# Fused retention and gated feed-forward: chunks taken two batch elements at a time, column-tiled Y and state, all inputs by software DMA

## The chip, the cores and the metric

The kernel runs on one core of one Trainium2 chip. The metric is device time in microseconds (us), the median of several executions (an execution over 1.5% above the fastest of its kernel counts as slow). A profile shows one execution, and its span (first to last instruction) is about 1.8 us shorter than the time of that execution.

Engines: PE does matmuls (PEld is its weight load), DVE, ACT and POOL (GpSimd) do elementwise work, SP (SyncE) issues DMAs. POOL also issues DMAs: the "software queue", as against SP's "hardware queue".

## The reference

```python
# q, k, v: (batch 4, heads 8, seq 768, head_dim 64) float32
gamma = 1.0 - 2.0 ** (-5.0 - np.arange(H))
for t in range(S):
    state = gamma * state + einsum('bhd,bhe->bhde', k[:, :, t], v[:, :, t])
    y[:, :, t] = scale * einsum('bhd,bhde->bhe', q[:, :, t], state)
x = y.transpose(0, 2, 1, 3).reshape(B * S, H * D)      # 3072 x 512
h = x @ w_in                                           # 512 -> 2048
out = (h * np.cos(h)) @ w_out                          # 2048 -> 512
```

Both kernels cut a sequence into 6 chunks of 128 positions. Within a chunk they form the masked scores of q and k, multiply by v and add what the 64x64 state of each head gives. The decay is folded into a scaling of q and of v by powers of gamma. There are 24 chunks; four of them make a 512-row group for the feed-forward part, so there are six groups.

## The kernel before

Per chunk: scale q (DVE) and v (POOL), transpose q and k on PE, scores, mask (DVE), Y, state. The stages of a chunk are issued between blocks of four feed-forward matmuls, one chunk per four blocks in and four blocks out ("[... ]" marks a cut):

```python
def load_chunk(ci):                 # k: software queue, cast to bf16; q, v: hardware queue
    for eng, t, src in ((nc.gpsimd, ks, k), (nc.sync, qf, q), (nc.sync, vf, v)):
        eng.dma_start(out=t[s], in_=src[b, :, ds(c * C, C)].rearrange("h t d -> t h d"))

def conv(ci):                       # qs = q * gq on DVE; vp = v * gk on POOL, zero-padded to 128 columns
    nc.vector.tensor_tensor(out=qs[n], in0=qf[s], in1=bc(gq), op=ALU.mult)
    nc.gpsimd.tensor_tensor(out=vout, in0=vf[s]..., in1=gk[...], op=ALU.mult)

def stage_y(ci):                    # 3 full-width matmuls for each pair of heads
    for a in range(HP):
        if c > 0:
            nc.tensor.matmul(yp[:, a, :], lhsT=stb[ci % 2][:, a, :], rhs=sq[ci % 3][:, 0, a, :], ...)
        for j in range(2):
            nc.tensor.matmul(yp[:, a, :], lhsT=vp[n][:, a, j, :], rhs=am[ci % 2][j][:, a, :], ...)

for g in range(NG + 1):
    for s in range(16):
        k4, r = divmod(s, 4)
        if g < NG: unit_f(g, s)               # 4 matmuls, Sin on ACT, multiply on DVE
        if g > 0:  unit_o(g - 1, k4, r)       # 4 matmuls
        ci = (g + 1) * GT + k4
        if ci < NT:
            if r == 0:   conv(ci); stage_t(ci)      # scaling and transposes in the same block
            elif r == 1: stage_a(ci)                # scores, mask
            elif r == 3: stage_y(ci); stage_s(ci); [... load_chunk(ci + GT)]
```

## Time and profile before

| | |
|---|---|
| Time | 276.5 us (276.05 to 278.29, 4 runs) |
| Span of the profile | 273.2 us |
| Start, to the first feed-forward matmul | 29.65 us |
| Group 0 (feed-forward-in and the attention of group 1) | 35.0 us |
| Groups 1 to 4 (in, out and attention) | 163.3 us, 20.4 us per two chunks |
| Tail (no attention left) | 45.2 us |

Lines of the page of the kernel before: span, busy time of each engine, and the span in 40 slices (a digit is the busy share in tenths; PEclk is the granted clock of PE), two DMA queues (packets, MB, share of 16 engines) and the engine shares of the chain of waits that ended last (followed back from the last instruction, at each step to what released it).

```profile
span 273.2 us, 3823 instructions
PE 217.3 (80%) x1480; PEld 111.6 (41%) x1504; DVE 129.1 (47%) x224; ACT 119.3 (44%) x172; POOL 53.6 (20%) x64
PE   0347469667988987988987988987988988999994
PEclk9999997989999999999999999999999999999999
DMA  9999999999275275175275274044000000100011
q1 hardware_dynamic: 53376, 18.88, 30.9%
q0 software_dynamic: 29184, 7.34, 27.1%
PE 67%; DVE 10%; ACT 8%; issue 3%; ACTq 0%; DVEq 0%
```

PE carries the chain, but its slices read 9, 8, 7: it pauses at a steady rhythm. DMA is saturated for the first ten slices (68 us) and only partly busy after that.

The stage table of the kernel before: a stretch, its length, then busy time of each engine in it, granted clock, DMA share (above 1 where packets overlap), GB/s.

```profile
0.00:29.65 29.65, 11.34 (x124) 9.11 (x125) 13.52 (x35) 8.08 (x12) 17.70 (x27) 1.00 1.31 193
29.65:64.65 35.00, 24.28 (x181) 12.28 (x185) 19.75 (x34) 18.40 (x25) 12.53 (x14) 0.90 1.38 180
64.65:227.96 163.31, 140.27 (x988) 71.53 (x1004) 84.73 (x141) 77.12 (x112) 23.41 (x24) 1.00 0.41 74
227.96:273.20 45.24, 41.39 (x188) 18.71 (x191) 11.06 (x16) 15.67 (x24) 0.00 (x0) 1.00 0.14 53
```

In groups 1 to 4 PE is idle for 163.31 - 140.27 = 23.0 us. The timeline of one chunk there (start, length, engine, line, instruction, and in brackets the idle time before it with what ended it) shows where:

```profile
126.67 0.69 ACT L212 ACTIVATE cosb_126<-bank_66,halfpi 128x512 bf16<-128x512 f32 x1 [0.50 <-PE bank_66 L209]
127.39 0.69 DVE L213 TENSOR_TENSOR gt_122<-bank_66,cosb_126 128x512 bf16<-128x512 f32 x1 [0.71 <-ACT cosb_126 L212]
128.00 0.68 DVE L138 TENSOR_TENSOR qs_107<-qf_87,gq 128x512 bf16<-128x512 f32 x1
128.74 0.40 PE L153 MATMUL bank_68<-ident,qs_107 128*128 128x128 bf16 x4 [1.24 <-DVE qs_107 L138]
```

DVE ran these in the order of issue. The scaling of q (L138) is issued behind the multiplication of the feed-forward block just begun (L213), which waits for that block's Sin (L212). So the transposes (L153) wait 1.24 us in every chunk, though this q had landed long ago, at 99.07 us.

Two lines of POOL's timeline at the start of the kernel before:

```profile
30.33 0.75 POOL L109 DMA_DIRECT2D w_out_sb<-in_moe_w_out_dram  x1 [0.61 <-DMA w_in_sb<-in_moe_w_in_dram]
32.78 0.95 POOL L101 DMA_DIRECT2D ks_89<-in_k_dram  x1 [0.64 <-DMA ks_93<-in_k_dram]
```

In these programs a software DMA waits until the eighth software DMA before it has landed (the built program uses eight completion semaphores in turn). No software DMA is issued before that landing, and the waits mostly end 0.3 us after it: in these two lines w_in had landed at 30.05 us and the k load at 32.49. The wait sits in POOL's own instruction stream, so POOL's elementwise work behind it waits too.

### The profile page before, as it was taken

What the parts mean: (1) busy time and instruction counts of PE and PEld (TensorE: products, weight loads), DVE (VectorE), ACT (ScalarE), POOL (GpSimd) and SP (SyncE); (2) the same over time, 40 slices, a digit from 0 to 9 for tenths busy, and PEclk for the clock granted to TensorE, in tenths of its full rate; (3) what the DMA queues carried; (4) which work ended last, traced back from release to release, by engine and by line L of the source; (5) the groups of instructions that cost most, each with busy time, mean ns of one, the idle gap of its engine ahead of it and who ended that gap; (6) DMA issues with size and microseconds to landing.
All of it is one profiled execution on the core that took longest, in us unless ns stands there. A gap on an engine that the chain in (4) does not pass through costs nothing.

```text
span 273.2 us, 3823 instructions
## 1 busy us (share of the span) xinstructions
PE 217.3 (80%) x1480; PEld 111.6 (41%) x1504; DVE 129.1 (47%) x224; ACT 119.3 (44%) x172; POOL 53.6 (20%) x64
## 2 busy tenths in 40 slices
PE   0347469667988987988987988987988988999994
PEld 0235234334534533434534534434534534444441
DVE  2636474556555553555554553654554653333200
ACT  2222455543544543544543644544544544444311
POOL 7527822225022022022012021101100000000000
PEclk9999997989999999999999999999999999999999
DMA  9999999999275275175275274044000000100011
GB/s 140 197 216 222 168 190 196 169 167 148 20 134 115 22 136 122 15 134 120 22 129 121 18 134 115 19 100 115 13 27 38 32 9 38 41 38 38 38 77 77
DMA packets 82577, 26.45 MB, mean 97 GB/s; under 512 B 75392, under 2 KB 79488, under 8 KB 82560
## 3 DMA queue, kind: packets, MB, share of 16 engines
q1 hardware_dynamic: 53376, 18.88, 30.9%
q0 software_dynamic: 29184, 7.34, 27.1%
q8 instruction: 11, 0.18, 0.3%
q14 instruction: 6, 0.05, 0.1%
HBM read 27.26 MB, written 6.29 MB: 123 GB/s over the span
## 4 chain that ended last, share of the span: by engine, by line
PE 67%; DVE 10%; ACT 8%; issue 3%; ACTq 0%; DVEq 0%
PE bank_69 L223 6%; PE bank_68 L209 5%; PE bank_65 L209 5%; PE bank_64 L209 5%; PE bank_67 L223 4%; PE bank_63 L223 4%; PE bank_66 L209 4%; PE bank_63 L209 4%; PE bank_67 L209 3%; PE bank_69 L209 3%; PE bank_65 L223 3%; PE bank_64 L223 3%; DVE gt_122 L213 3%; PE bank_66 L223 3%; ACT cosb_124 L212 3%
## 5 line engine op out<-in xcount | busy, mean ns | idle before, releaser
L209 PEld LDWEIGHTS <-w_in_sb 128*128 128x128 bf16 x384 | 34.9, 99 | 38.7 <-issue 7.2
L223 PEld LDWEIGHTS <-gt_122 128*128 128x128 bf16 x192 | 18.8, 98 | 22.6
L223 PEld LDWEIGHTS <-gt_123 128*128 128x128 bf16 x192 | 18.8, 98 | 22.7
L223 PE MATMUL bank_69<-w_out_sb,gt_122 128*128 128x512 bf16 x63 | 16.2, 379 | 0.1
L153 PEld LDWEIGHTS <-qs_105 128*128 128x128 bf16 x32 | 2.0, 106 | 25.3 <-DVE qs_105 L138 25.3
L223 PE MATMUL bank_63<-w_out_sb,gt_123 128*128 128x512 bf16 x48 | 11.8, 379 | 0.0
L223 PE MATMUL bank_64<-w_out_sb,gt_123 128*128 128x512 bf16 x48 | 11.8, 379 | 0.0
L209 PE MATMUL bank_68<-xt_121,w_in_sb 128*128 128x512 bf16 x40 | 10.8, 379 | 1.0 <-ACT xt_121 L202 0.7
L185 DVE CAST stb_119<-st_ps 64x256 bf16<-64x256 f32 x24 | 10.1, 421 | 2.8 <-PE st_ps L181 2.1
L209 PE MATMUL bank_64<-xt_121,w_in_sb 128*128 128x512 bf16 x42 | 10.9, 380 | 0.1
L209 PE MATMUL bank_66<-xt_120,w_in_sb 128*128 128x512 bf16 x36 | 10.1, 401 | 0.4 <-issue 0.3
L209 PE MATMUL bank_65<-xt_120,w_in_sb 128*128 128x512 bf16 x34 | 9.2, 385 | 0.6 <-ACT xt_120 L202 0.5
L212 ACT ACTIVATE cosb_126<-bank_66,halfpi 128x512 bf16<-128x512 f32 x8 | 5.5, 688 | 7.4 <-PE bank_66 L209 7.4
L209 PE MATMUL bank_69<-xt_120,w_in_sb 128*128 128x512 bf16 x33 | 8.6, 380 | 0.2
L209 PE MATMUL bank_65<-xt_121,w_in_sb 128*128 128x512 bf16 x31 | 8.2, 379 | 0.5 <-ACT xt_121 L202 0.5
L185 DVE CAST stb_118<-st_ps 64x256 bf16<-64x256 f32 x16 | 6.7, 421 | 3.7 <-PE st_ps L181 3.4
L223 PE MATMUL bank_67<-w_out_sb,gt_122 128*128 128x512 bf16 x31 | 8.2, 379 | 0.1
L223 PE MATMUL bank_65<-w_out_sb,gt_122 128*128 128x512 bf16 x32 | 8.2, 379 | 0.0
L223 PE MATMUL bank_67<-w_out_sb,gt_123 128*128 128x512 bf16 x32 | 8.2, 379 | 0.0
L223 PE MATMUL bank_66<-w_out_sb,gt_122 128*128 128x512 bf16 x32 | 8.2, 379 | 0.0
L153 PEld LDWEIGHTS <-qs_107 128*128 128x128 bf16 x32 | 1.9, 101 | 15.4 <-DVE qs_107 L138 15.4
L212 ACT ACTIVATE cosb_124<-bank_65,halfpi 128x512 bf16<-128x512 f32 x8 | 5.5, 688 | 6.2 <-PE bank_65 L209 6.2
(391 smaller groups left out, 491.7 us busy)
## 6 DMA issues: line engine op xcount, KB each, us to landing
w_in_sb<-in_moe_w_in_dram POOLq DMA_DIRECT2D x4, 512.0 KB, 8.9
w_out_sb<-in_moe_w_out_dram POOLq DMA_DIRECT2D x4, 512.0 KB, 18.1
out_dram<-ob_127 SPq DMA_DIRECT2D x6, 256.0 KB, 2.1
out_dram<-ob_128 SPq DMA_DIRECT2D x6, 256.0 KB, 2.1
out_dram<-ob_129 SPq DMA_DIRECT2D x6, 256.0 KB, 2.1
out_dram<-ob_130 SPq DMA_DIRECT2D x6, 256.0 KB, 2.1
qf_81<-in_q_dram SPq DMA_DIRECT2D x3, 256.0 KB, 3.4
vf_97<-in_v_dram SPq DMA_DIRECT2D x3, 256.0 KB, 4.2
```

Of the source, the lines that this page charges most:

```text
L153: nc.tensor.transpose(tr[:, w, a, :], src[:, 2 * a : 2 * a + 2, :], ident)
L185: nc.vector.tensor_copy(out=stb[(ci + 1) % 2][ts(j, 64), :, ts(j, 64)], in_=st_ps[ts(j, 64), :, ts(j, 64)])
L209: nc.tensor.matmul(bank, lhsT=w_in_sb[:, i, ts(f, 128)], rhs=xt[g % 2][:, i, :], start=(i == 0), stop=(i == KIN - 1))
L212: nc.scalar.activation(out=cb, in_=bank, func=AF.Sin, bias=halfpi)
L213: nc.vector.tensor_tensor(out=gt[g % 2][:, f, :], in0=bank, in1=cb, op=ALU.mult)
L223: nc.tensor.matmul(bank, lhsT=gt[g % 2][:, f, ts(j, 128)], rhs=w_out_sb[:, f, :], start=(f == 0), stop=(f == KOUT - 1))
```

## The change

The intent: handle the same chunk of two batch elements as one pair, so that each stage is issued once per eight blocks; spread the stages (transposes one block after scaling, Y four blocks after scores); write Y and state of the two heads of a pair into the two column halves of the array, so that they can run side by side without zero padding; and take q's scaling from DVE by giving it to POOL. q, k and v are now all loaded by POOL's software queue as float32; k is cast by DVE (by ACT for the first two pairs).

```diff
-    def load_chunk(ci):
-        for eng, t, src in ((nc.gpsimd, ks, k), (nc.sync, qf, q), (nc.sync, vf, v)):
-            eng.dma_start(out=t[s], in_=src[b, :, ds(c * C, C)]...)
+    def load_pair(p):
+        for t, src in ((qf, q), (kf, k), (vf, v)):
+            for b in range(2):
+                nc.gpsimd.dma_start(out=t[p % PRE][:, b], in_=src[2 * bp + b, :, ds(c * C, C)]...)
 [... stage_y: two half-width products for the state, two for v ...]
-                nc.tensor.matmul(yp[:, a, :], lhsT=stb[ci % 2][:, a, :], ...)
-                nc.tensor.matmul(yp[:, a, :], lhsT=vp[n][:, a, j, :], ...)
+                for j in range(2):
+                    nc.tensor.matmul(yp[ts(j, 64), a, :], lhsT=stb[p % 2][:, b, a, ts(j, 64)], ...)
+                for j in range(2):
+                    nc.tensor.matmul(yp[ts(j, 64), a, :], lhsT=vs[n][:, b, 2 * a + j, :], ...)
 [... state likewise: st_ps[ts(j, 64), b, a, :], 64 columns of 64 ...]
 [... start: two pairs loaded, w_in, the two pairs' attention, then: ...]
+    load_pair(2)
+    load_pair(3)
+    stage_y(1)
+    for r in range(4):
+        load_w_out(r)
+    load_pair(4)
+    def conv(p):
+        conv_q(p, nc.gpsimd)
+        conv_k(p, False)            # DVE
+        conv_v(p, nc.gpsimd)
 [... main loop, hf, r = divmod(s, 8) ...]
+                if r == 0:
+                    conv(p)
+                elif r == 1:
+                    stage_t(p)
+                elif r == 2:
+                    todo = stage_a(p)
+                    stage_m(p, todo[0])
+                elif r == 3:
+                    stage_m(p, todo[1])
+                elif r == 6:
+                    stage_y(p)      # and state
+                    if p + 3 < NP:
+                        load_pair(p + 3)
```

More of the change, by code (lines that the diff above doesn't have):

```diff
@@ L49 @@
     KOUT = DF // 128
-    GT = 4
-    NT = B * NC
-    NG = NT // GT
-    PRE = 8
+    NP = B // 2 * NC
+    NG = NP // 2
+    PRE = 5
     scale = 1.0 / math.sqrt(D)
@@ L67 @@
     banks = Banks([psum.tile([128, 512], FP32, name=f"bank{i}") for i in range(7)])
-    st_ps = psum.tile([128, HP, 128], FP32, name="st_ps")
+    st_ps = psum.tile([128, 2, HP, D], FP32, name="st_ps")
     ident = sb([128, 128], BF16, "ident")
@@ L80 @@
     w_out_sb = sb([128, KOUT, DM], BF16, "w_out_sb")
-    qf = [sb([128, H, D], FP32, f"qf{i}") for i in range(PRE)]
-    ks = [sb([128, H, D], BF16, f"ks{i}") for i in range(PRE)]
-    vf = [sb([128, H, D], FP32, f"vf{i}") for i in range(PRE)]
+    qf = [sb([128, 2, H, D], FP32, f"qf{i}") for i in range(PRE)]
+    kf = [sb([128, 2, H, D], FP32, f"kf{i}") for i in range(PRE)]
+    vf = [sb([128, 2, H, D], FP32, f"vf{i}") for i in range(PRE)]
     NB = 3
-    qs = [sb([128, H, D], BF16, f"qs{i}") for i in range(NB)]
-    vp = [sb([128, HP, 2, 128], BF16, f"vp{i}") for i in range(NB)]
-    sq = [sb([128, 2, HP, 128], BF16, f"sq{i}") for i in range(3)]
-    am = [[sb([128, HP, 128], BF16, f"am{i}_{j}") for j in range(2)] for i in range(2)]
-    stb = [sb([128, HP, 128], BF16, f"stb{i}") for i in range(2)]
-    xt = [sb([128, KIN, GT * C], BF16, f"xt{i}") for i in range(2)]
-    gt = [sb([128, KOUT, GT * C], BF16, f"gt{i}") for i in range(2)]
-    cosb = [sb([128, GT * C], BF16, f"cosb{i}") for i in range(3)]
-    ob = [sb([128, DM], FP32, f"ob{i}") for i in range(4)]
-    def load_chunk(ci):
-        b, c = divmod(ci, NC)
-        s = ci % PRE
-        for eng, t, src in ((nc.gpsimd, ks, k), (nc.sync, qf, q), (nc.sync, vf, v)):
-            eng.dma_start(out=t[s], in_=src[b, :, ds(c * C, C)].rearrange("h t d -> t h d"))
+    qs = [sb([128, 2, H, D], BF16, f"qs{i}") for i in range(NB)]
+    ks = [sb([128, 2, H, D], BF16, f"ks{i}") for i in range(NB)]
+    vs = [sb([128, 2, H, D], BF16, f"vs{i}") for i in range(NB)]
+    qkt = [sb([128, 2, 2, HP, 128], BF16, f"qkt{i}") for i in range(NB)]
+    am = [[[sb([128, HP, 128], BF16, f"am{i}_{b}_{j}") for j in range(2)]
+           for b in range(2)] for i in range(2)]
+    stb = [sb([128, 2, HP, 128], BF16, f"stb{i}") for i in range(2)]
+    xt = [sb([128, KIN, 4 * C], BF16, f"xt{i}") for i in range(2)]
+    gt = [sb([128, KOUT, 4 * C], BF16, f"gt{i}") for i in range(2)]
+    cosb = [sb([128, 4 * C], BF16, f"cosb{i}") for i in range(3)]
+    ob = [sb([128, DM], FP32, f"ob{i}") for i in range(4)]
+    def load_pair(p):
+        bp, c = divmod(p, NC)
+        for t, src in ((qf, q), (kf, k), (vf, v)):
+            for b in range(2):
+                nc.gpsimd.dma_start(
+                    out=t[p % PRE][:, b],
+                    in_=src[2 * bp + b, :, ds(c * C, C)].rearrange("h t d -> t h d"))
     def load_w_in(r):
@@ L111, in load_w_out @@
             in_=moe_w_out[ts(r, 512), :].rearrange("(f p) m -> p f m", p=128))
-    for ci in range(GT):
-        load_chunk(ci)
     nc.gpsimd.iota(pos, pattern=[[C, NC]], base=1, channel_multiplier=1,
                    allow_small_or_imprecise_dtypes=True)
+    load_pair(0)
+    make_identity(nc, ident)
     nc.vector.memset(lnsc, math.log(scale))
     nc.vector.memset(halfpi, math.pi / 2.0)
+    nc.vector.memset(mask, 1.0)
     for h in range(H):
@@ L125 @@
     nc.scalar.activation(out=gk, in_=lgp, func=AF.Exp, scale=-1.0)
-    make_identity(nc, ident)
-    nc.vector.memset(mask, 1.0)
     nc.gpsimd.affine_select(out=mask, in_=mask, compare_op=ALU.is_ge, fill=0.0,
                             base=0, pattern=[[1, 128]], channel_multiplier=-1)
-    for t in vp + stb:
+    for t in stb:
         nc.vector.memset(t, 0.0)
-    def conv(ci):
-        c = ci % NC
-        s, n = ci % PRE, ci % NB
-        bc = lambda g: g[:, c, :].unsqueeze(2).to_broadcast([128, H, D])
-        nc.vector.tensor_tensor(out=qs[n], in0=qf[s], in1=bc(gq), op=ALU.mult)
-        vout = vp[n].rearrange("p a j (l e) -> p a (j l) e", l=2)[:, :, 0:4:3, :]
-        nc.gpsimd.tensor_tensor(
-            out=vout,
-            in0=vf[s].rearrange("p (a j) e -> p a j e", j=2),
-            in1=gk[:, c, :].rearrange("p (a j) -> p a j", j=2).unsqueeze(3).to_broadcast(
-                [128, HP, 2, D]),
-            op=ALU.mult)
@@ L147, in stage_t, with bc @@
-    def stage_t(ci):
-        n = ci % NB
-        bank = banks.take()
-        tr = bank.bitcast(BF16).rearrange("p (w a t) -> p w a t", w=2, a=HP)
-        for w, src in enumerate((qs[n], ks[ci % PRE])):
-            for a in range(HP):
-                nc.tensor.transpose(tr[:, w, a, :], src[:, 2 * a : 2 * a + 2, :], ident)
-        nc.scalar.copy(out=sq[ci % 3], in_=tr)
-        banks.give(bank)
-    def stage_a(ci):
-        s = sq[ci % 3]
-        bk = [banks.take(), banks.take()]
-        ap = [t.rearrange("p (a t) -> p a t", a=HP) for t in bk]
-        for a in range(HP):
-            for j in range(2):
-                po = 64 * j
-                nc.tensor.matmul(ap[j][:, a, :], lhsT=s[po : po + 64, 1, a, :],
-                                 rhs=s[po : po + 64, 0, a, :], tile_position=(po, 0))
+    def bc(g, c):
+        return g[:, c, :].unsqueeze(2).to_broadcast([128, H, D])
@@ new lines, in conv_q, with conv_v, conv_k @@
+    def conv_q(p, eng):
+        for b in range(2):
+            eng.tensor_tensor(out=qs[p % NB][:, b], in0=qf[p % PRE][:, b],
+                              in1=bc(gq, p % NC), op=ALU.mult)
+    def conv_v(p, eng):
+        for b in range(2):
+            eng.tensor_tensor(out=vs[p % NB][:, b], in0=vf[p % PRE][:, b],
+                              in1=bc(gk, p % NC), op=ALU.mult)
+    def conv_k(p, on_act):
+        if on_act:
+            nc.scalar.copy(out=ks[p % NB], in_=kf[p % PRE])
+        else:
+            nc.vector.tensor_copy(out=ks[p % NB], in_=kf[p % PRE])
@@ new lines, in stage_t, with qt @@
+    def stage_t(p):
+        n = p % NB
+        for b in range(2):
+            bank = banks.take()
+            tr = bank.bitcast(BF16).rearrange("p (w a t) -> p w a t", w=2, a=HP)
+            for w, src in enumerate((qs[n], ks[n])):
+                for a in range(HP):
+                    nc.tensor.transpose(tr[:, w, a, :], src[:, b, 2 * a : 2 * a + 2, :], ident)
+            nc.scalar.copy(out=qkt[n][:, b], in_=tr)
+            banks.give(bank)
+    def qt(n, b, a):
+        return qkt[n][:, b, 0, a, :]
@@ new lines, in kt, with stage_a @@
+    def kt(n, b, a):
+        return qkt[n][:, b, 1, a, :]
+    def stage_a(p):
+        n = p % NB
+        todo = []
+        for b in range(2):
+            bk = [banks.take(), banks.take()]
+            ap = [t.rearrange("p (a t) -> p a t", a=HP) for t in bk]
+            for a in range(HP):
+                for j in range(2):
+                    po = 64 * j
+                    nc.tensor.matmul(ap[j][:, a, :], lhsT=kt(n, b, a)[po : po + 64, :],
+                                     rhs=qt(n, b, a)[po : po + 64, :],
+                                     tile_position=(po, 0))
+            todo.append((b, bk, ap))
+        return todo
@@ L166, in stage_a, with stage_m, stage_y @@
+    def stage_m(p, item):
+        b, bk, ap = item
         for j in range(2):
             nc.vector.tensor_tensor(
-                out=am[ci % 2][j], in0=ap[j],
+                out=am[p % 2][b][j], in0=ap[j],
                 in1=mask.unsqueeze(1).to_broadcast([128, HP, 128]), op=ALU.mult)
             banks.give(bk[j])
-    def vnat(n, a):
-        return vp[n][:, a].rearrange("p j (l e) -> p (j l) e", l=2)[:, 0:4:3, :]
-    def stage_s(ci):
-        c = ci % NC
+    def stage_y(p):
+        c = p % NC
+        n = p % NB
+        for b in range(2):
+            bank = banks.take()
+            yp = bank.rearrange("p (a t) -> p a t", a=HP)
+            for a in range(HP):
+                if c > 0:
+                    for j in range(2):
+                        nc.tensor.matmul(
+                            yp[ts(j, 64), a, :], lhsT=stb[p % 2][:, b, a, ts(j, 64)],
+                            rhs=qt(n, b, a), start=True, stop=False,
+                            skip_group_check=True)
+                for j in range(2):
+                    nc.tensor.matmul(
+                        yp[ts(j, 64), a, :], lhsT=vs[n][:, b, 2 * a + j, :],
+                        rhs=am[p % 2][b][j][:, a, :], start=(c == 0), stop=True,
+                        skip_group_check=True)
+            nc.scalar.copy(out=xt[(p // 2) % 2][:, :, ts(2 * (p % 2) + b, C)], in_=yp)
+            banks.give(bank)
@@ L177, in stage_s @@
         if c == NC - 1:
             return
-        n = ci % NB
-        for a in range(HP):
-            nc.tensor.matmul(st_ps[:, a, :], lhsT=ks[ci % PRE][:, 2 * a : 2 * a + 2, :],
-                             rhs=vnat(n, a), start=(c == 0 and a == 0),
-                             stop=True, skip_group_check=True)
-        for j in range(2):
-            nc.vector.tensor_copy(out=stb[(ci + 1) % 2][ts(j, 64), :, ts(j, 64)],
-                                  in_=st_ps[ts(j, 64), :, ts(j, 64)])
@@ L188, in stage_y @@
-    def stage_y(ci):
-        c = ci % NC
-        n = ci % NB
-        bank = banks.take()
-        yp = bank.rearrange("p (a t) -> p a t", a=HP)
-        for a in range(HP):
-            if c > 0:
-                nc.tensor.matmul(yp[:, a, :], lhsT=stb[ci % 2][:, a, :],
-                                 rhs=sq[ci % 3][:, 0, a, :], start=True, stop=False,
-                                 skip_group_check=True)
-            for j in range(2):
-                nc.tensor.matmul(yp[:, a, :], lhsT=vp[n][:, a, j, :],
-                                 rhs=am[ci % 2][j][:, a, :], start=(c == 0 and j == 0),
-                                 stop=(j == 1), skip_group_check=True)
-        nc.scalar.copy(out=xt[(ci // GT) % 2][:, :, ts(ci % GT, C)], in_=yp)
-        banks.give(bank)
+        for b in range(2):
+            for a in range(HP):
+                for j in range(2):
+                    h = 2 * a + j
+                    nc.tensor.matmul(
+                        st_ps[ts(j, 64), b, a, :], lhsT=ks[n][:, b, h, :],
+                        rhs=vs[n][:, b, h, :], start=(c == 0 and b == 0 and a == 0),
+                        stop=True, skip_group_check=True)
@@ L206, in unit_f @@
+        for j in range(2):
+            nc.vector.tensor_copy(out=stb[(p + 1) % 2][ts(j, 64), :, :, ts(j, 64)],
+                                  in_=st_ps[ts(j, 64)])
     def unit_f(g, f):
@@ L228, in unit_o @@
             banks.give(bank)
-            nc.sync.dma_start(out=out[ds((g * GT + j) * C, C), :], in_=o)
-    for ci in range(GT + 2):
-        if ci < GT:
-            conv(ci)
-            load_w_in(ci)
-            stage_t(ci)
-        if 1 <= ci < GT + 1:
-            stage_a(ci - 1)
-        if 2 <= ci:
-            stage_y(ci - 2)
-            stage_s(ci - 2)
-    for ci in range(GT, 2 * GT):
-        load_chunk(ci)
+            bp, c = divmod(2 * g + j // 2, NC)
+            nc.sync.dma_start(out=out[ds((2 * bp + j % 2) * S + c * C, C), :], in_=o)
+    load_pair(1)
+    for r in range(2):
+        load_w_in(r)
+    conv_q(0, nc.vector)
+    conv_k(0, True)
+    conv_v(0, nc.gpsimd)
+    stage_t(0)
+    for r in range(2, 4):
+        load_w_in(r)
+    m0 = stage_a(0)
+    conv_q(1, nc.vector)
+    conv_k(1, True)
+    conv_v(1, nc.gpsimd)
+    for it in m0:
+        stage_m(0, it)
+    stage_t(1)
+    stage_y(0)
+    m1 = stage_a(1)
+    for it in m1:
+        stage_m(1, it)
+    load_pair(2)
+    load_pair(3)
+    stage_y(1)
     for r in range(4):
         load_w_out(r)
+    load_pair(4)
[3 more added lines that the diff above has]
+        conv_v(p, nc.gpsimd)
+    todo = []
     for g in range(NG + 1):
         for s in range(16):
-            k4, r = divmod(s, 4)
+            hf, r = divmod(s, 8)
+            p = 2 * (g + 1) + hf
             if g < NG:
@@ L253 @@
             if g > 0:
-                unit_o(g - 1, k4, r)
-            ci = (g + 1) * GT + k4
-            if ci < NT:
+                unit_o(g - 1, *divmod(s, 4))
+            if p < NP:
                 if r == 0:
-                    conv(ci)
-                    stage_t(ci)
+                    conv(p)
                 elif r == 1:
-                    stage_a(ci)
+                    stage_t(p)
+                elif r == 2:
+                    todo = stage_a(p)
+                    stage_m(p, todo[0])
                 elif r == 3:
-                    stage_y(ci)
-                    stage_s(ci)
-                    if ci + GT < NT:
-                        load_chunk(ci + GT)
+                    stage_m(p, todo[1])
[3 more added lines that the diff above has]
+                        load_pair(p + 3)
 _INS = ['q', 'k', 'v', 'moe_w_in', 'moe_w_out']
```

## The prediction

> **What bounds it now.** The chain of waits is 67% PE; PE is busy 80% (busy table). The PE timeline splits the 273.2 us span into a start until the first feed-forward matmul (29.65), group 0 (to 64.65), groups 1 to 4 (to 227.96: 163.3 us, 20.4 us per two chunks) and a tail of 45.2 us left alone.
>
> In groups 1 to 4 two chunks cost PE about 13.8 us of feed-forward (16 blocks of four 216 ns matmuls), 0.9 transposes, 0.65 scores, 1.8 Y and state: 17.1. The remaining 3.3 us are waits. The largest: transposes wait 1.24 us per chunk for DVE's scaling of q (timeline, wait list), which sits behind the block just issued.
>
> In the first 68 us DMA is saturated (slices); group 0 shows 2.1 to 2.3 us waits for q per chunk and a halved clock at 42-46 and 60-63.
>
> **Steady gain.** q's scaling joins v's on POOL, which runs ahead; the cast of k stays on DVE but is issued one block (1.7 us) before the transposes; Y comes four blocks after scores. So the 1.24 us waits go, and the 0.7 us wait for xt at group starts. POOL gets six DMA issues of 0.9 us and four 1.03 us multiplications per pair: 9.5 of about 17 us, no bound. DMA: 6144 packets per pair at the roughly 1000 per us that the packet records show for the software queue alone: 6 us, no bound.
>
> Column tiling: Y goes from 24 full to 32 half matmuls per pair, state from 8 to 16 of half the columns. Paired they would save 0.6 us; but the Trainium skill, "TensorEngine Tiling (Array Packing)" (Restrictions; Key Properties), says that column tiling disables Fast Weight Load and that a mode switch drains the array (this trace has no column tile to check). I count no gain: 1.7 us. Expected 17.3 us per pair, 138 for groups 1 to 4: 25 us saved, nearly all waits.
>
> **Start loss.** All loads are in one software queue in order. Each such DMA waits for the eighth before it to land (trace: w_out at 30.3 waited for w_in; the built program too), and POOL computes in order behind them. Pairs 0 and 1 should land by about 17.5 us and the first feed-forward matmul start near 25. But the scaling of pair 2 stands in POOL's order behind pairs 2, 3, w_out and pair 4: 38 DMAs, whose last is issued about 45 (1 us per load, 2.6 per weight block, from the packet records). PE does two blocks, then idles from about 27 to 47, restarts at low clock, and finishes group 0 around 70: 5 us later than now.
>
> **Sum.** 70 + 138 + 45 = 253 to 254 us span; times exceed it by about 3.5. Predicted 257 us, range 247 to 268 (8 in 10). Faster by over 2%: 0.92; within 2%: 0.06; slower: 0.02.
>
> **Checks.** Right if: one PE idle of 15 to 22 us ended by POOL's q scaling between 25 and 50 us; group 1 starts at 63 to 76; pairs take 16.9 to 18.2 us; transposes stop waiting for q; tail 45 us.
>
> **Wrong if:** 256-byte software packets run well below 1000 per us (start 10 us worse); column tiles serialize with slow weight loads (1.3 us per pair worse); four score banks or DVE order create new waits; POOL is slowed by DVE; or POOL is not held at the start (up to 15 us better).

## The result and the profile after

The changed kernel takes 254.07 us (253.85 to 254.5, 4 runs) against 276.5: the ratio is 0.918, with a 95% interval of 0.914 to 0.922. Ratios here are the mean time of one kernel's fast runs over that of the other's of the same rounds, so not quite the ratio of the quoted medians.

The same lines of the page of the changed kernel:

```profile
span 252.3 us, 4113 instructions
PE 204.9 (81%) x1640; PEld 107.4 (43%) x1664; DVE 119.1 (47%) x191; ACT 120.1 (48%) x174; POOL 116.8 (46%) x132
PE   0447400099798999999999999999999999999994
PEclk9999755569999999999999999999999999999999
DMA  4999999999979689779301110111011101111122
q0 software_dynamic: 9984, 23.07, 44.1%
PE 67%; POOL 15%; DMA 10%; issue 5%; DVE 1%; ACT 0%; POOLq 0%; ACTq 0%
```

The rhythm of pauses is gone: PE's slices are 9s. In its place there are three zeros near the start, with a lowered clock, and the chain now runs through POOL for 15% and DMA for 10% of the span. The busy share of PE went from 80% to just 81%, an average over a better middle and a worse start. The stage table, cut at the same events as before:

```profile
0.00:25.99 25.99, 10.39 (x145) 8.16 (x146) 11.45 (x28) 9.88 (x14) 24.54 (x34) 0.97 0.96 187
25.99:72.94 46.95, 22.45 (x219) 12.27 (x224) 18.09 (x30) 17.31 (x24) 35.99 (x40) 0.73 1.09 220
72.94:207.08 134.14, 130.59 (x1090) 68.30 (x1105) 77.78 (x119) 76.59 (x112) 56.23 (x59) 1.00 0.35 90
207.08:252.30 45.22, 41.44 (x190) 18.71 (x191) 11.75 (x17) 16.28 (x26) 0.00 (x0) 1.00 0.14 53
```

| Stage | before | after | difference |
|---|---|---|---|
| Start | 29.65 | 25.99 | -3.7 |
| Group 0 | 35.00 | 46.95 | +11.9 |
| Groups 1 to 4 | 163.31 | 134.14 | -29.2 |
| Tail | 45.24 | 45.22 | 0 |

In groups 1 to 4 PE's idle time fell from 23.0 to 3.6 us (134.14 - 130.59): two thirds of the 29.2 us. The other third is counted as busy: a matmul before a wait is busy to its modelled end (0.38 us, where in a stream the next starts after 0.22), so a wait costs more than its idle time; and Y and state take less. One wait for DVE is left in these groups, 1.01 us for k's cast in pair 4. The transposes of a steady pair no longer wait; this is pair 7 in the timeline of the changed kernel, where DVE's cast of k (L153) is under way before PE has finished its feed-forward blocks:

```profile
126.03 0.68 DVE L153 CAST ks_100<-kf_88 128x1024 bf16<-128x1024 f32 x1
127.10 0.39 PE L162 MATMUL bank_69<-ident,qs_97 128*128 128x128 bf16 x4
127.32 0.39 PE L162 MATMUL bank_69<-ident,ks_100 128*128 128x128 bf16 x4
```

And Y runs in pairs: the two column halves start together every 55 ns or so (timeline of the changed kernel, Y of one chunk):

```profile
121.17 0.22 PE L208 MATMUL bank_69<-am_0_0_108,vs_102 128*64 128x128 bf16 x1
121.17 0.22 PE L208 MATMUL bank_69<-am_0_1_109,vs_102 128*64 128x128 bf16 x1
121.22 0.22 PE L208 MATMUL bank_69<-am_0_0_108,vs_102 128*64 128x128 bf16 x1
121.23 0.22 PE L208 MATMUL bank_69<-am_0_1_109,vs_102 128*64 128x128 bf16 x1
```

Group 0 is where time was lost. PE's timeline of the changed kernel there:

```profile
28.18 0.59 PE L232 MATMUL bank_66<-xt_118,w_in_sb 128*128 128x512 bf16 x2
51.00 0.40 PE L162 MATMUL bank_67<-ident,qs_98 128*128 128x128 bf16 x2 [22.23 <-POOL qs_98 L141]
```

POOL's timeline of the same kernel, just before that wait ends:

```profile
46.11 0.88 POOL L103 DMA_DIRECT2D vf_95<-in_v_dram  x1 [1.25 <-DMA w_out_sb<-in_moe_w_out_dram]
48.99 0.88 POOL L103 DMA_DIRECT2D vf_95<-in_v_dram  x1 [2.00 <-DMA w_out_sb<-in_moe_w_out_dram]
49.89 1.05 POOL L141 TENSOR_TENSOR qs_98<-qf_83,gq 128x512 bf16<-128x512 f32 x1
```

PE waits 22.2 us for the scaled q of pair 2 (qs_98). Its input had landed by 32.1 us: POOL's second issue of a k load for pair 3, at 32.14, waited for exactly that landing. But POOL comes to the scaling (L141) only after issuing the last load of pair 4, which waits for a w_out load to land.

### The profile page after: what moved, and what is told of

It is laid out like the page before. It is cut to its first block, busy times and chain, and to the rows that moved or that the text cites. A ratio compares the mean times of both kernels' runs of the same rounds, so it can differ in the third digit from the quotient of the medians.

```text
span 252.3 us, 4113 instructions
## 1 busy us (share of the span) xinstructions
PE 204.9 (81%) x1640; PEld 107.4 (43%) x1664; DVE 119.1 (47%) x191; ACT 120.1 (48%) x174; POOL 116.8 (46%) x132
## 4 chain that ended last, share of the span: by engine, by line
PE 67%; POOL 15%; DMA 10%; issue 5%; DVE 1%; ACT 0%; POOLq 0%; ACTq 0%
PE bank_66 L246 14%; PE bank_63 L246 6%; PE bank_65 L232 5%; DMA vf_93<-in_v_dram 5%; PE bank_64 L232 5%; DMA w_out_sb<-in_moe_w_out_dram 5%; PE bank_69 L232 4%; PE bank_67 L232 4%; PE bank_68 L232 4%; PE bank_67 L246 4%; PE bank_63 L232 3%; PE bank_68 L246 3%; PE bank_69 L246 3%; POOL vs_103 L146 1%; POOL vs_102 L146 1%
## 5 line engine op out<-in xcount | busy, mean ns | idle before, releaser
L232 PEld LDWEIGHTS <-w_in_sb 128*128 128x128 bf16 x384 | 36.0, 99 | 40.8 <-issue 2.0
L246 PEld LDWEIGHTS <-gt_120 128*128 128x128 bf16 x192 | 18.8, 98 | 22.6
L246 PEld LDWEIGHTS <-gt_121 128*128 128x128 bf16 x192 | 18.8, 98 | 22.6
L246 PE MATMUL bank_66<-w_out_sb,gt_120 128*128 128x512 bf16 x96 | 24.6, 379 | 0.0
L162 PE MATMUL bank_67<-ident,qs_98 128*128 128x128 bf16 x8 | 1.0, 264 | 22.2 <-POOL qs_98 L141 22.2
L235 ACT ACTIVATE cosb_122<-bank_65,halfpi 128x512 bf16<-128x512 f32 x14 | 9.6, 687 | 14.5 <-PE bank_65 L232 14.5
L246 PE MATMUL bank_66<-w_out_sb,gt_121 128*128 128x512 bf16 x64 | 16.4, 379 | 0.0
L246 PE MATMUL bank_63<-w_out_sb,gt_120 128*128 128x512 bf16 x63 | 16.2, 379 | 0.1
L163 ACT COPY qkt_107<-bank_67 128x1024 bf16<-128x1024 bf16 x2 | 2.0, 1012 | 23.2 <-PE bank_67 L162 23.2
L162 PEld LDWEIGHTS <-qs_98 128*128 128x128 bf16 x32 | 2.4, 106 | 23.6 <-POOL qs_98 L141 22.9
L246 PE MATMUL bank_67<-w_out_sb,gt_121 128*128 128x512 bf16 x48 | 11.8, 379 | 0.0
L236 DVE TENSOR_TENSOR gt_120<-bank_69,cosb_124 128x512 bf16<-128x512 f32 x3 | 2.0, 683 | 19.9 <-ACT cosb_124 L235 19.9
L232 PE MATMUL bank_69<-xt_119,w_in_sb 128*128 128x512 bf16 x44 | 11.3, 379 | 0.0
L225 DVE CAST stb_117<-st_ps 64x512 bf16<-64x512 f32 x12 | 8.2, 687 | 5.7 <-PE st_ps L220 5.5
L235 ACT ACTIVATE cosb_124<-bank_64,halfpi 128x512 bf16<-128x512 f32 x9 | 6.2, 687 | 9.7 <-PE bank_64 L232 9.7
L232 PE MATMUL bank_63<-xt_118,w_in_sb 128*128 128x512 bf16 x40 | 10.3, 379 | 0.0
L232 PE MATMUL bank_65<-xt_119,w_in_sb 128*128 128x512 bf16 x34 | 8.8, 379 | 0.3 <-issue 0.3
L232 PE MATMUL bank_67<-xt_119,w_in_sb 128*128 128x512 bf16 x34 | 8.8, 379 | 0.3 <-issue 0.3
L232 PE MATMUL bank_64<-xt_119,w_in_sb 128*128 128x512 bf16 x34 | 8.8, 379 | 0.3 <-issue 0.3
L232 PE MATMUL bank_65<-xt_118,w_in_sb 128*128 128x512 bf16 x28 | 8.2, 405 | 0.9 <-issue 0.7
L246 PE MATMUL bank_68<-w_out_sb,gt_120 128*128 128x512 bf16 x32 | 8.2, 379 | 0.0
L246 PE MATMUL bank_69<-w_out_sb,gt_121 128*128 128x512 bf16 x32 | 8.2, 379 | 0.0
```

The lines of the kernel that those rows point to most:

```text
L162: nc.tensor.transpose(tr[:, w, a, :], src[:, b, 2 * a : 2 * a + 2, :], ident)
L163: nc.scalar.copy(out=qkt[n][:, b], in_=tr)
L225: nc.vector.tensor_copy(out=stb[(p + 1) % 2][ts(j, 64), :, :, ts(j, 64)], in_=st_ps[ts(j, 64)])
L232: nc.tensor.matmul(bank, lhsT=w_in_sb[:, i, ts(f, 128)], rhs=xt[g % 2][:, i, :], start=(i == 0), stop=(i == KIN - 1))
L235: nc.scalar.activation(out=cb, in_=bank, func=AF.Sin, bias=halfpi)
L236: nc.vector.tensor_tensor(out=gt[g % 2][:, f, :], in0=bank, in1=cb, op=ALU.mult)
```

## The experiments

Each experiment ran with three rounds beside the kernel before. The changed kernel itself was not run again beside them; the kernel before had medians of 276.2 to 277.2 in these rounds against 276.5, so a difference of 1 us in time is not read. "A steady pair" below is the mean of six, from the start of the transposes of pair 5 to that of pair 11 in the PE timeline: 20.39 us in the kernel before, 16.62 in the changed one, and 16.62 again in e3, e7 (both runs) and e9, so its noise is small. My theory had two parts: the steady gain is removed waits (plus, once seen, paired column halves), and the start loss is POOL's program order. The rivals: column tiling or POOL alone made the gain, and DMA bandwidth made the loss.

### e1_serial: the order of Y and state matmuls

```diff
-            for a in range(HP):
-                [... for j in range(2): state;  for j in range(2): v]
+            for j in range(2):
+                for a in range(HP):
+                    [... state, v of this half]
```

> The changed kernel with only the order of the Y and state matmuls altered: all of column half 0 first, then all of half 1, so that neighbours never sit in different halves. Same instructions, same bytes. Theory 1 (neighbours in different column halves run at the same time, and this is worth about 1 us per pair of chunks): Y and state take about 0.9 to 1.1 us more per pair, a steady pair goes from 16.8 to 17.7 or 17.9 us, the time from 254.1 to about 262. Theory 2 (the steady gain is removed waits only, column tiling is neutral): within 1.5 us of 254.1.

257.62 us, correct; a steady pair 16.89 us, 0.27 more. That fits neither theory, because the edit did not do what it was meant to do. From the PE timeline of this run, Y (L203, L207) and state (L219):

```profile
139.43 0.22 PE L207 MATMUL bank<-am,vs 128*64 128x128 bf16 x1
139.49 0.25 PE L203 MATMUL bank<-qkt,stb 128*64 128x128 bf16 x2
...
140.25 0.22 PE L219 MATMUL st_ps<-vs,ks 128*64 128x64 bf16 x1
140.36 0.22 PE L203 MATMUL bank<-qkt,stb 128*64 128x128 bf16 x1
140.41 0.22 PE L207 MATMUL bank<-am,vs 128*64 128x128 bf16 x1
```

The first few run alone, then each has a neighbour from the other half, which in the program comes four matmuls later (eight instructions with their weight loads). Even a state matmul (L219) starts before Y matmuls that precede it in the program. Here PE pulled work for the idle half forward. So program order is a weak tool for stopping the overlap; the test had to be made otherwise.

### e5_onehalf: every Y matmul into column half 0

```diff
-                            yp[ts(j, 64), a, :], [...]     # state and v
+                            yp[ts(0, 64), a, :], [...]
```

> The changed kernel with every Y matmul writing column half 0, so no two can run side by side; same instructions and count, the result is wrong on purpose (half of Y is never written, half overwritten). The serial order tried before (e1) did not stop the overlap: its records show the other half's matmuls pulled forward. Theory 1 (halves run side by side and save PE time): Y takes 32 x 56 ns = 1.8 us per pair instead of 0.9, a steady pair takes 17.5 to 17.8 us instead of 16.75, time 261 to 265. Theory 2 (half-width matmuls are cheap by themselves, about 29 ns each, pairing or not): within 2 us of e1's 257.6 or of 254.1.

262.14 us, wrong result as intended. A steady pair takes 17.44 us, 0.82 more (a little under the stated 17.5). From its PE timeline (pairs of lines of x2, 0.11 us apart):

```profile
141.76 0.28 PE L208 MATMUL bank<-am,vs 128*64 128x128 bf16 x2
141.87 0.28 PE L203 MATMUL bank<-qkt,stb 128*64 128x128 bf16 x2
```

Two half-width matmuls in the same half take 0.11 us, 56 ns each; in different halves, 56 ns together. Theory 1 holds: a half-width matmul alone is as dear as a full one, and the halves run side by side.

### e6_fully: Y full-width again

```diff
-    conv_v writes vs [128, 2, H, D];  Y = 4 half-width products for each pair of heads
+    conv_v writes vp [128, 2, HP, 2, 128], zero-padded;  Y = 3 full-width products, as before
```

> The changed kernel with Y as full-width matmuls on block-diagonal and zero-padded weights, as the kernel before had it (24 per pair); state stays in halves. Theory 1 (column tiling of Y saves PE time in proportion to slots): 24 x 56 ns = 1.34 instead of 0.9 us, less a mode switch: a steady pair 17.0 to 17.2 us, time 256 to 259. Theory 2 (column tiling bought nothing in the total): 253 to 255.

258.11 us, correct; a steady pair takes 17.05 us. Against the version before, column tiling of Y is therefore worth 0.43 us per pair: 24 slots of 56 ns become 16. Its 32 narrower weight loads cost nothing visible. The switch to half-width does cost something: in the changed kernel the first half-width matmul of Y starts 0.309 us after the last feed-forward one, a full-width one in e6 and in the kernel before 0.216 us after. In e6 the same 0.09 us stand between Y and state instead.

### e4_qdve: q's scaling back on DVE, in place

```diff
     def conv(p):
-        conv_q(p, nc.gpsimd)
+        conv_q(p, nc.vector)
```

> The changed kernel with the scaling of q back on DVE (in place, one block before the transposes). Theory 1 (the waits went because POOL runs ahead): transposes wait again, for DVE, by 0.7 to 0.9 us per pair, a steady pair takes 17.5 to 17.8 us; at the start pair 2's transposes come near 35 us but Y of pair 2 then waits for v on POOL until about 52; time 250 to 254. Theory 2 (one block of distance alone removed the waits): steady pairs stay at 16.8 and the time is 246 to 248.

257.84 us, correct. A steady pair takes 17.35 us, 0.72 more (the first theory said 17.5 to 17.8). The wait list of PE in this run (waiting instruction, what it waited for, total us, times, longest):

```profile
PE bank L162 <- DVE ks L153: 9.6, 10, 3.3
PE bank L208 <- POOL vs L146: 7.7, 1, 7.7
PE bank L162 <- DVE qs L141: 3.8, 4, 1.7
```

With q's two multiplications ahead of it in DVE's order, k's cast is late again (0.50 us in each of the later pairs). So POOL's part in the steady gain is real, but not most of it. At the start the theory's shape held and its size did not: pair 2's transposes came at 31.4 us (q) and 35.1 (k), then Y of pair 2 waited until 51.05 for v, which is still scaled on POOL behind the loads. Group 1 began only some 3 us earlier, and the time was 4 us above the expected range.

### e8_close: transposes in the same block as scaling and cast

```diff
                 if r == 0:
                     conv(p)
-                elif r == 1:
                     stage_t(p)
```

> The changed kernel with the transposes of a pair put back right behind its scaling and cast (same block), nothing else moved. Theory 1 (issuing the cast one block before the transposes is what removed DVE's wait): transposes wait 0.9 to 1.2 us per pair for k's cast, a steady pair takes 17.6 to 18.0 us, time 261 to 265. Theory 2 (only POOL's running ahead with q mattered): a wait under 0.3 us and 254 to 256.

270.46 us, correct: most of the gain is lost (ratio 0.975 to the kernel before, interval 0.968 to 0.982, so whether it is still 2% faster is unclear). That is 5 us above the expected range. A steady pair takes 18.19 us on average, 1.57 more (17.93 in the last two). The wait appears where expected, in its PE timeline:

```profile
116.71 0.40 PE L162 MATMUL bank<-ident,ks 128*128 128x128 bf16 x4 [1.02 <-DVE ks L153]
134.97 0.40 PE L162 MATMUL bank<-ident,ks 128*128 128x128 bf16 x4 [1.79 <-DVE ks L153]
```

Three of the six pairs wait 1.02 us, as predicted, and three 1.72 to 1.79, which was not; the mean is 1.39. Counted from the start of one matmul to the start of the next, these waits cost 1.56 us per pair, which is all of the 1.57. Why some are longer has not been taken apart. The distance of one block between cast and transposes is the largest single piece of the steady gain that I isolated.

### e2_order: POOL's scaling ahead of the w_out and pair 4 loads

```diff
     load_pair(2); load_pair(3); stage_y(1)
+    conv_q(2, nc.gpsimd); conv_v(2, nc.gpsimd)
     for r in range(4): load_w_out(r)
+    conv_q(3, nc.gpsimd); conv_v(3, nc.gpsimd)
     load_pair(4)
 [... in the loop, POOL's scaling of pair p + 1 in place of pair p ...]
```

> The changed kernel with POOL's scaling of pairs 2 and 3 issued ahead of the w_out and pair 4 loads (before and after the four w_out loads), and each later pair's scaling one load earlier; nothing else moved. Theory 1 (the 22 us idle of PE is POOL's program order, not missing data): transposes of pair 2 start near 38 instead of 51 us, group 1 near 60 instead of 73, time about 242. Theory 2 (DMA bandwidth sets the start; the idle moves to a later wait for pair 3, w_out or pair 4): time 249 or more.

242.38 us, correct, as the first theory said to within half a microsecond. The same wait in the PE timeline of this run:

```profile
36.62 0.61 PE L162 MATMUL bank<-ident,qs 128*128 128x128 bf16 x4 [7.43 <-POOL qs L141]
```

The 22.2 us wait is 7.4, and feed-forward-out begins at 59.99 instead of 73.80 us. The bytes and the queue are the same, so these 14.8 us were POOL's order, not bandwidth. The 7.4 us that remain are not all missing data either: POOL's scaling still stands behind the loads of pair 3, the last of them issued at 34.61 us.

### e3_hwload: q, k, v by the hardware queue

```diff
-                nc.gpsimd.dma_start(
+                nc.sync.dma_start(
```

> The changed kernel with q, k and v loaded by the sync engine's hardware queue instead of the software queue; still f32. Theory 1 (POOL held by the software queue's eight-deep waits is the cause of the start loss): the idle before pair 2's transposes shrinks, but weights now compete with q, k, v from the start, so the first feed-forward comes later, about 30 to 36 us; time 246 to 254, steady pairs unchanged at 16.8. Theory 2 (the software queue's order, inputs ahead of weights, is worth more than POOL's freedom): slower than 256.

245.42 us (just under the stated 246 to 254), correct: 8.7 us better than the changed kernel, with no other edit. A steady pair is unchanged (16.62). The first feed-forward matmul comes at 32.16 us, 6 us later, as weights now compete from the start, but the 22 us wait is gone. What is left from there on is shorter waits for v, the first of them before that feed-forward matmul (PE timeline):

```profile
29.52 0.32 PE L208 MATMUL bank<-am,vs 128*64 128x128 bf16 x2 [2.93 <-POOL vs L146]
49.82 0.32 PE L208 MATMUL bank<-am,vs 128*64 128x128 bf16 x2 [5.72 <-POOL vs L146]
```

So of the change's parts, the software queue for q, k and v was a loss in the order in which it came.

### e7_hworder and e9_hworder2: both repairs together

```diff
 [e3's edit, and on POOL:]
+    conv_v(0); load_w_in(0); conv_v(1); load_w_in(1); load_w_in(2)
+    conv_q(2); conv_v(2); load_w_in(3); load_w_out(0)
+    conv_q(3); conv_v(3); load_w_out(1); load_w_out(2); load_w_out(3)
 [... the loop as in e2; e9 issues w_out 1 before conv_q(3) and w_out 2 before conv_v(3)]
```

Each weight load stands behind the scaling of a pair, so it cannot be issued before that pair has landed.

> A version meant to beat both: q, k, v by the sync engine's hardware queue, and POOL's order such that each weight load stands behind the scaling of the pair before it, so weights do not starve the inputs; POOL's scaling of a pair one load earlier, as in e2. Expected if e2's and e3's gains add: no PE idle over 4 us after the first feed-forward matmul, first feed-forward near 23 to 27, group 1 near 50 to 54 us, time 230 to 236. If DMA is the floor of the start whatever the order: 240 or more.

235.53 us (234.73 to 238.18), correct, ratio 0.851 to the kernel before: faster than both kernels. The first feed-forward matmul is at 24.42 us, feed-forward-out begins at 50.80. One wait over 4 us was left, not none, for w_out (PE timeline of e7):

```profile
56.78 1.87 PE L246 MATMUL bank<-w_out_sb,gt 128*128 128x512 bf16 x4 [4.09 <-DMA w_out_sb<-in_moe_w_out_dram]
```

> e7 with the w_out loads issued earlier: w_out 1 ahead of the scaling of pair 3, w_out 2 between its q and v, w_out 3 after. If e7's 4.1 us wait of the first feed-forward-out matmuls for w_out is only a matter of POOL's order, it falls below 1.5 us and the time to 231 to 234. If DMA is the floor of the start now, the wait moves to Y of pair 3 or to pair 4 and the time stays within 2 us of 235.5.

237.42 us (236.0 to 239.24), correct, and e7 repeated beside it:

> e7 unchanged, as the neighbour of e9 on the same chip: 235 to 236.

235.48 us. The ranges of e9 and e7 overlap, so neither is shown to be faster. In e9 the wait for w_out is gone from the list, and this has come instead (its PE timeline, then its POOL timeline):

```profile
51.32 0.32 PE L208 MATMUL bank<-am,vs 128*64 128x128 bf16 x2 [4.40 <-POOL vs L146]
50.22 1.04 POOL L146 TENSOR_TENSOR vs<-vf,gk 128x512 bf16<-128x512 f32 x1 [5.60 <-DMA vf<-in_v_dram]
```

The wait only moved to v of pair 3, and POOL in turn waited for its landing: that load was issued at 34.77 us and landed at 50.06. DMA is at 90% or more in nearly all of the first fifteen slices of e7's page (to about 88 us), so I read DMA as what now limits the start, whatever the order. That is inferred from the moved wait and this landing; no run with less to load has shown it.

## Why the prediction was right

The time lay 3 us under the predicted 257 and well inside the range. Point by point:

- **Waits removed in groups 1 to 4: right.** The 1.24 us waits and the 0.7 us waits at group starts are gone. e8 puts waits of 1.02 to 1.79 us back, e4 one of 0.50.
- **Column tiling "no gain: 1.7 us": wrong, and the term that made groups 1 to 4 better than predicted** (16.77 us per pair over the whole stretch against 17.3, outside the stated 16.9 to 18.2). I gave too much weight to the skill's restrictions in "TensorEngine Tiling (Array Packing)", Tile-to-Partition Mapping. Halves do run side by side, as that page's Key Properties say of tiles, and Y is worth 0.43 us per pair (e6). If Fast Weight Load was off, its cost did not show: two half-width matmuls with their loads took the 56 ns of one full-width matmul. The switch cost 0.09 us where half-width work begins, too little to cancel the gain.
- **The start loss: right in cause, short in size.** One PE idle, ended by POOL's scaling of q, in 25 to 51 us; 22.2 us against a stated 15 to 22, group 1 at 72.9 against 70. The mis-sized term is a load's time: 1.0 us predicted from packet records of the kernel before, about 1.2 measured (a 256 KB load at 218 GB/s, in packets of 4096 bytes where 256 were assumed). Pair 4's last load was issued at 48.99 instead of 45: it waited for a landing at 48.37 us, and 24 such loads, each 0.2 us longer than assumed, had to land before. PE restarted at half the clock, as predicted (51 to 55 us: 0.50). e2 shows that the order on POOL is the cause.
- **The tail: right**, 45.2 us before and after.
- **The difference of time and span**: 1.8 us where 3.5 was assumed. The 3.5 set the median time before against the span of a profile whose own execution took only 274.98 us.

The sizes offset each other: groups 1 to 4 gained 4 us more, the start lost 3 us more than predicted, and the smaller difference of time and span gave 2. The mechanisms were mostly right; that the total came within 3 us is luck, because misses of 3 to 4 us cancelled.

What stays open: of the 3.77 us that a steady pair gained (20.39 - 16.62), undoing single parts gives back 0.43 (Y's halves), 0.72 (q on POOL) and 1.57 (distance), 2.72 in sum. These need not add up, and the rest (one wait shared by two chunks, the group-start wait, the state's halves) had no run of its own. The traces narrow it down: over the same six pairs, counted from one matmul's start to the next, the transposes' waits cost 2.81 us per pair in the kernel before (2.48 of it idle) and none in the changed one. So three quarters of the gain are these waits; how they divide among distance, POOL and pairing is known only from e8 and e4.

## What to carry to other kernels

When an engine executes in order, as DVE and POOL did here, look at what stands ahead of an instruction in its stream, not just at what the instruction needs: moving a cast by one block and a multiplication to a less loaded engine was worth more here (1.57 and 0.72 us per pair) than faster matmuls (0.43). An engine that both issues DMAs and computes can hold its computing behind DMA waits, as POOL did for most of 22 us; place the scaling that PE needs next ahead of loads that are needed later. And if a busy share hardly moves (80 to 81%), cut the span into stages: here 29 us were gained in one and 12 lost in another, and most of the loss could be had back by reordering.

## What the Trainium skill lacked or had wrong

- "TensorE: Matmul & The Clock Gate", Part 3, The mechanism, says that matmuls are strict FIFO and start in program order in all its traces. Here they do not across column halves: in e1 a state matmul started at 140.25 us, before Y matmuls that precede it in the program (140.36, 140.41).
- The same page, LDWEIGHTS, gives columns / 1.2 ns, an estimate of 53 ns for 64 columns. In the changed kernel's state block at 121.5 us two loads of 64 columns start together, one for each half, and the next two mostly 32 ns later: 16 loads start within 0.25 us (each record is about 0.11 us long).
- "TensorEngine Tiling (Array Packing)", Tile-to-Partition Mapping, Restrictions, names the loss of Fast Weight Load but no size, and Key Properties the drain at a mode switch, also without one. The drain: 0.09 us from full to half width (0.309 against 0.216 us, changed kernel and e6). The loss: with 128 columns of moving data it cost nothing visible (56 ns per pair of half-width matmuls, e5 beside the changed kernel).
- "DMA: Bandwidth & Descriptors", SWDGE vs HWDGE vs iDMA, says that packets are preferably up to 4096 bytes. The trace agrees: the software queue moved the 256-byte rows of q, k and v in 4096-byte packets, at 218 GB/s; loads that cast moved in packets of 128 bytes (k before) and 1024 (weights). No page has this rate for 256-byte rows; the hardware queue alone, in 256-byte packets, reached the same 218 GB/s (about 865 packets per us, e9 from 7 to 13 us).
- The same page, Queues, rings and completion order, says that engines take turns between queues packet by packet. The trace agrees and shows what that does to small packets: beside weight packets, in the kernel before from 38 to 47 us, each queue got about 150 packets per us, so the 256-byte queue fell to about 38 GB/s. No page draws that consequence.
- No page tells of the wait of a software DMA for the eighth before it; it is in the built program, and cost 14 us here together with POOL's order (51.00 against 36.62 us in e2).
